# Windowed attention over half-blocks of 64 keys in eight array tiles, with the value products in two turns around a score batch

## Chip, cores and metric

The kernel runs on one core of one Trainium2 chip. The metric is the device time of one execution in microseconds (us), median over the runs. One run of the kernel before (388.53 us, the first of all) is left out. The profile of a run is one more execution, and its span (first to last instruction) is some 2 us shorter than the time.

## The reference

A layer norm of x (2048 rows of 512), then two branches whose results are added to x: attention with 32 heads of 16 dimensions, where a query sees itself and the 255 keys before it, and a gated product without a nonlinearity.

```python
xn = _layernorm(x)
qkv = (xn @ wqkv)                                  # 512 -> 3*512, 32 heads of 16
scores = einsum("bhqd,bhkd->bhqk", q, k) * 16**-0.5
mask = (i - j >= 0) & (i - j < 256)                # i: query, j: key
p = softmax(where(mask, scores, -1e9))
a = einsum("bhqk,bhkd->bhqd", p, v) ... @ wo
h = (xn @ w_gate) * (xn @ w_up)                    # 512 -> 1792
return x + a + h @ w_down
```

## The kernel before

The sequence is cut into four chunks of 512 rows (T), the heads into four quarters (c) of eight heads, and those into two parities (par) of four heads (e). TensorE is kept busy by interleaving attention with "fillers", the large products (projections, gate, up, down, output projection), all 128x128 by 512 columns. A schedule on cost estimates decides how many fillers stand between two score batches.

A score batch multiplies blocks of 128 keys with the queries that can see them, for four heads at once: each head has 16 or 32 rows of the array (a 32x128 tile) and writes its 512 columns to a PSUM bank of its own. Per chunk, quarter and parity there are six key blocks with 1, 2, 3, 3, 2 and 1 query blocks, packed into three batches. ScalarE takes the exp of a whole batch (128 x 2048), GpSimd zeroes what the mask hides, block by block. A value product then takes three batches: 128 keys deep, 17 columns per head (16 values and a column of ones for the softmax sum), four heads side by side (128x32 tiles).

```python
GROUPS = (            # (key block, first query block, last, column)
    ((-2, 0, 0, 0), (0, 0, 2, 128)),
    ((-1, 0, 1, 0), (2, 2, 3, 256)),
    ((1, 1, 3, 0), (3, 3, 3, 384)),
)

def scores(self, T, c, par, i):
    S = self.ps_s.tile([128, 4, 512], F32, tag="S", name="S")          # four banks
    for kb, q0, q1, col in parts:
        for e in range(4):
            nc.tensor.matmul(S[:, e, col:col + n], lhsT=K[rows of e, ..128 keys..],
                             rhs=Q[rows of e, .. n queries ..], tile_position=(32 * e, 0), ...)
    nc.scalar.activation(out=P[:, :, lo:hi], in_=S[:, :, lo:hi], func=ACT.Exp, scale=0.25)
    # ... one gpsimd.affine_select per block on the diagonal (q == kb) or the window's end (q == kb + 2)

def values(self, T, c, par):
    acc = self.accb                                                    # a bank of its own
    # ... for each of the three batches, key block and e:
    #     matmul(acc[32e:32e+17, queries], lhsT=V[128 keys, 17], rhs=P, tile_position=(0, 32e))
    nc.vector.transpose(out=at, in_=acc[:])
    nc.vector.reciprocal(out=rz[:], in_=at[:, :, 16])
    nc.vector.tensor_tensor(out=self.on[:, :, par, :], in0=at[:, :, 0:16], in1=rz..., op=ALU.mult)
    if par == 1:
        nc.vector.transpose(out=self.OT[T][:, c, :], in_=self.on...)

for g, s in enumerate(steps):            # 96 batches
    fill(-1, g)
    self.scores(*s)
    values(g - LAG)                      # LAG = 2: values of the batch two before, if it was the last of three
    fill(total * done_w / sum(weight), g)
```

The large products go through three more PSUM banks (`ps_m`), which VectorE or ScalarE must empty before they are used again.

The softmax here doesn't subtract the row's maximum and nothing guards it: scores larger than these inputs give would overflow.

## Time and profile before

| | before |
|---|---|
| time, median of the runs | 285.11 us |
| span of the profile | 282.7 us |
| TensorE busy | 96% |
| VectorE, ScalarE, GpSimd busy | 66%, 65%, 58% |
| first score batch starts | 13.64 us |
| last score batch starts | 265.43 us |

Part 1 of the page of the kernel before: busy us, share of the span and instruction count of each engine.

```profile
PE 270.2 (96%) x2380; PEld 113.9 (40%) x2396; DVE 186.5 (66%) x338; ACT 182.9 (65%) x121; POOL 162.6 (58%) x284
```

Busy time of TensorE (PE) is no proof of a full array, since matmuls are pipelined: the record of a full-array matmul lasts 0.38 us. The start times tell more: the next one starts 0.216 us after it. The stretch view of the kernel before, from the first scores to the first scores of chunk 1, and from there to the last score batch (columns: stretch, length, then busy us and count for each engine):

```profile
13.60:66.05 52.45, 48.67 (x400) 19.59 (x401) 42.67 (x77) 36.56 (x28) 31.61 (x56) 1.00 0.41 122
66.05:265.40 199.35, 197.03 (x1811) 80.93 (x1823) 133.48 (x237) 136.80 (x79) 124.00 (x208) 1.00 0.06 15
```

TensorE has hardly a gap after 66 us, and no other engine comes near. Before that, in the first chunk, it loses nearly 4 us (stretch minus busy time), and VectorE is 81% busy.

The timeline of TensorE in the kernel before, one score batch and one value product (columns: start, us, engine, line, operation, tiles, shapes, count):

```profile
127.72 0.40 PE L222 MATMUL S<-Q,Ko 32*128 32x256 bf16 x8
128.04 0.83 PE L255 MATMUL accb<-P,V 128*17 128x128 bf16 x24
128.81 1.47 PE L164 MATMUL vp<-Wqkv,xnT 128*128 128x512 bf16 x6
```

From start to start the batch takes 0.33 us and the value product 0.77. Another 0.09 us passes between the last full-array matmul's 0.216 us and the first score matmul (read from single starts). The second column is not the cost: it includes the tail of the pipeline. Streaming itself takes 0.417 ns per column, an estimate; so 512 columns take 0.213 us, 128 take 53 ns and 64 take 27 ns.

The first chunk, where a batch follows a value product without fillers between, in the timeline of the kernel before:

```profile
35.27 0.29 PE L222 MATMUL S<-Q,Ko 32*128 32x256 bf16 x4
35.49 0.67 PE L255 MATMUL accb<-P,V 128*17 128x384 bf16 x16
36.74 0.40 PE L222 MATMUL S<-Q,Ko 32*128 32x384 bf16 x8 [0.59 <-ACT P L230]
```

The product of 35.49 should end the step at 36.09. The next batch waits until 36.74 because the exp of the batch before still reads the score banks.

### The profile page before, as it was taken

What the parts mean: (1) busy time and instruction counts of PE and PEld (TensorE: products, weight loads), DVE (VectorE), ACT (ScalarE), POOL (GpSimd) and SP (SyncE); (2) the same over time, 40 slices, a digit from 0 to 9 for tenths busy, and PEclk for the clock granted to TensorE, in tenths of its full rate; (3) what the DMA queues carried; (4) which work ended last, traced back from release to release, by engine and by line L of the source; (5) the groups of instructions that cost most, each with busy time, mean ns of one, the idle gap of its engine ahead of it and who ended that gap; (6) DMA issues with size and microseconds to landing.
All of it is one profiled execution on the core that took longest, in us unless ns stands there. A gap on an engine that the chain in (4) does not pass through costs nothing.

```text
span 282.7 us, 5799 instructions
## 1 busy us (share of the span) xinstructions
PE 270.2 (96%) x2380; PEld 113.9 (40%) x2396; DVE 186.5 (66%) x338; ACT 182.9 (65%) x121; POOL 162.6 (58%) x284
## 2 busy tenths in 40 slices
PE   7999898989999999999999999999999999999994
PEld 6433333334344434443444344434434444433441
DVE  6377989958675777775853688875753367877122
ACT  3667666687576666668757676767776666756601
POOL 5146666765676665556586756465656566655510
PEclk9999999999999999999999999999999999999999
DMA  6999510100022100000011110000001000000002
GB/s 199 379 371 349 98 21 19 21 0 3 0 58 56 40 0 2 1 2 0 2 39 38 56 21 0 2 2 1 2 0 37 21 21 1 2 0 2 0 0 74
DMA packets 17161, 13.73 MB, mean 49 GB/s; under 512 B 7024, under 2 KB 17136, under 8 KB 17136
## 3 DMA queue, kind: packets, MB, share of 16 engines
q1 hardware_dynamic: 16848, 13.18, 15.5%
q8 instruction: 18, 0.29, 0.4%
q10 hardware_dynamic: 288, 0.20, 0.2%
q14 instruction: 7, 0.06, 0.1%
HBM read 9.70 MB, written 2.10 MB: 42 GB/s over the span
## 4 chain that ended last, share of the span: by engine, by line
PE 79%; DVE 10%; ACT 5%; issue 2%; DMA 1%; POOL 1%; ACTq 0%; DVEq 0%
PE psd L308 17%; PE gp L282 15%; PE up L293 14%; PE S L222 10%; PE accb L255 7%; PE qkp L176 6%; ACT P L230 5%; PE psd L313 4%; PE vp L164 4%; DVE at L266 2%; DVE OT L272 2%; DVE on L269 1%; DVE Q L187 1%; DVE hT L297 1%; DVE K L181 1%
## 5 line engine op out<-in xcount | busy, mean ns | idle before, releaser
L230 ACT ACTIVATE P<-S 128x2048 bf16<-128x2048 f32 (+2 forms) x96 | 170.1, 1772 | 79.1 <-PE S L222 68.5
L235 POOL TENSOR_SCALAR_AFFINE_SELECT P<-P 128x512 bf16<-128x512 bf16 x128 | 82.4, 644 | 57.5 <-ACT P L230 57.5
L239 POOL TENSOR_SCALAR_AFFINE_SELECT P<-P 128x512 bf16<-128x512 bf16 x112 | 72.9, 651 | 39.8 <-ACT P L230 39.5
L282 PE MATMUL gp<-xnT,Wg 128*128 128x512 bf16 x224 | 59.7, 380 | 1.2 <-DVE hT L297 1.1
L293 PE MATMUL up<-xnT,Wu 128*128 128x512 bf16 x224 | 60.4, 380 | 0.2 <-DVE gsb L287 0.2
L308 PE MATMUL psd<-Wd,hT 128*128 128x512 bf16 x215 | 53.1, 380 | 1.4 <-issue 0.8
L266 DVE STREAM_TRANSPOSE at<-accb 128x512 f32<-128x512 f32 x32 | 22.8, 713 | 38.9 <-PE accb L255 38.8
L297 DVE TENSOR_TENSOR hT<-up,gsb 128x512 bf16<-128x512 f32 x56 | 38.4, 686 | 7.8 <-PE up L293 5.2
L287 DVE CAST gsb<-gp 128x512 bf16<-128x512 f32 x56 | 38.2, 683 | 6.4 <-PE gp L282 6.1
L282 PEld LDWEIGHTS <-Wg 128*128 128x128 bf16 x224 | 20.0, 98 | 27.7 <-issue 7.1
L308 PEld LDWEIGHTS <-hT 128*128 128x128 bf16 x224 | 20.3, 98 | 26.7 <-issue 5.2
L176 PE MATMUL qkp<-xnT,Wqkv 128*128 128x512 bf16 x128 | 30.7, 380 | 0.0
L293 PEld LDWEIGHTS <-Wu 128*128 128x128 bf16 x224 | 19.8, 98 | 26.0 <-issue 5.9
L255 PE MATMUL accb<-P,V 128*17 128x384 bf16 (+2 forms) x704 | 25.4, 276 | 0.0
L329 DVE TENSOR_TENSOR y<-psd,x 128x512 bf16<-128x512 f32 (+1 forms) x15 | 9.9, 665 | 22.8 <-PE psd L313 21.5
L222 PE MATMUL S<-Q,Ko 32*128 32x256 bf16 (+2 forms) x352 | 18.4, 275 | 2.0 <-ACT P L230 2.0
L222 PE MATMUL S<-Q,K 16*128 16x256 bf16 (+2 forms) x352 | 18.4, 275 | 1.0 <-ACT P L230 0.7
L255 PEld LDWEIGHTS <-V 128*17 128x17 bf16 x704 | 13.8, 90 | 8.7 <-issue 5.5
L176 PEld LDWEIGHTS <-Wqkv 128*128 128x128 bf16 x128 | 11.3, 98 | 14.6 <-issue 2.9
L181 DVE CAST K<-qkp 128x512 bf16<-128x512 f32 x16 | 11.0, 687 | 8.5 <-PE qkp L176 8.4
L313 PE MATMUL psd<-Wo,OT 128*128 128x512 bf16 x61 | 16.0, 379 | 0.5 <-issue 0.5
L269 DVE TENSOR_TENSOR on<-at,rz 128x256 bf16<-128x256 f32 x32 | 15.4, 482 | 1.1
(39 smaller groups left out, 138.9 us busy)
## 6 DMA issues: line engine op xcount, KB each, us to landing
Wg<-in_B_w_gate_dram SPq DMA_DIRECT2D x2, 896.0 KB, 10.8
Wu<-in_B_w_up_dram SPq DMA_DIRECT2D x2, 896.0 KB, 11.9
Wd<-in_B_w_down_dram SPq DMA_DIRECT2D x1, 1792.0 KB, 16.4
out_dram<-y SPq DMA_DIRECT2D x14, 128.0 KB, 1.7
Wqkv<-in_A_wqkv_dram SPq DMA_DIRECT2D x3, 512.0 KB, 5.7
x<-in_A_x_dram SPq DMA_DIRECT2D x1, 1024.0 KB, 11.1
x<-in_A_x_dram SPq DMA_DIRECT2D x1, 512.0 KB, 11.1
Wo<-in_A_wo_dram SPq DMA_DIRECT2D x1, 512.0 KB, 16.3
```

The lines of the kernel that those rows point to most:

```text
L176: nc.tensor.matmul(ps[:], lhsT=self.Wqkv[:, k, lo:lo + 128], rhs=self.xnT[T][:, :, k, :], start=(k == 0), stop=(k == 3))
L222: nc.tensor.matmul(S[:, e, col:col + n], lhsT=(self.Ko if par else self.K)[U][rows, c, 128 * j:128 * j + 128], rhs=self.Q[T][rows, c, 128 ...
L230: nc.scalar.activation(out=P[:, :, lo:hi], in_=S[:, :, lo:hi], func=ACT.Exp, scale=0.25)
L235: nc.gpsimd.affine_select(out=P[:, :, j:j + 128], in_=P[:, :, j:j + 128], pattern=[[0, 4], [1, 128]], compare_op=ALU.is_ge, fill=0.0, base ...
L239: nc.gpsimd.affine_select(out=P[:, :, j:j + 128], in_=P[:, :, j:j + 128], pattern=[[0, 4], [-1, 128]], compare_op=ALU.is_gt, fill=0.0, bas ...
L255: nc.tensor.matmul(acc[32 * e:32 * e + 17, 128 * q0:128 * q0 + n], lhsT=self.V[U][:, v, 8 * c + 2 * e + par, 0:17], rhs=P[:, e, col:col + ...
L266: nc.vector.transpose(out=at.rearrange("p b r -> p (b r)"), in_=acc[:])
L282: nc.tensor.matmul(ps[:], lhsT=self.Wg[:, k, 128 * f:128 * f + 128], rhs=self.xnT[T][:, :, k, :], start=(k == 0), stop=(k == 3))
L287: nc.vector.tensor_copy(out=self.gsb[:], in_=ps[:])
L293: nc.tensor.matmul(ps[:], lhsT=self.Wu[:, k, 128 * f:128 * f + 128], rhs=self.xnT[T][:, :, k, :], start=(k == 0), stop=(k == 3))
L297: nc.vector.tensor_tensor(out=self.hT[T][:, f, :], in0=ps[:], in1=self.gsb[:], op=ALU.mult)
L308: nc.tensor.matmul(self.psd, lhsT=self.hT[T][:, f, 128 * b:128 * b + 128], rhs=self.Wd[:, f, :], start=(f == 0), stop=False)
```

## The change

The aim is to spend fewer columns on keys outside the window, and to use the array in eight tiles at a time.

- Keys go in half-blocks of 64. One needs 320 query columns, where a block of 128 needs 384. Per chunk, quarter and parity that is 2560 columns of 64 keys, 2.5 full batches, where there were 3: 76 batches in all for 96 (batch Z serves both parities).
- Scores use 32x64 tiles: four heads times two half-blocks at once. Values use 64x32 tiles: four heads times two halves of 64 rows.
- The two row halves must not write to one PSUM bank at once. The Trainium skill, "TensorEngine Tiling (Array Packing)", Gotcha 1, says that different row tiles cannot access the same bank simultaneously. So both parities are computed together, in two turns: in turn 0 the even half-blocks write to the accumulator of parity 0 and the odd ones to that of parity 1, in turn 1 the other way round. A tiny ScalarE read of each accumulator (a "mark") makes turn 1 wait for the end of turn 0, and a score batch stands between to hide the wait.
- The accumulators are two of the (now four) rotating banks; the score banks are one lasting tile, cleared at the start and used for the last down sums.
- The masks are 64-row cuts on GpSimd; those of batch Y, parity 1, become multiplications on VectorE in chunks 1 to 3.

```diff
+STEPS = {            # (half-block, column, first query, queries); two in a step run side by side
+    "X": (((0, 0, 0, 320), (1, 0, 64, 320)), ((-2, 320, 0, 192), (5, 320, 320, 192))),
+    "Y": (((2, 0, 128, 320), (3, 0, 192, 320)), ((6, 320, 384, 128), (-3, 384, 0, 128)),
+          ((-4, 448, 0, 64), (7, 320, 448, 64))),
+    "Z": (((4, 0, 256, 256), (-1, 0, 0, 256)),),
+}
 ...
-        self.ps_a = pool("ps_a", 1, space=bass.MemoryType.PSUM)
-        self.ps_m = pool("ps_m", 3, space=bass.MemoryType.PSUM)
+        self.ps_m = pool("ps_m", 4, space=bass.MemoryType.PSUM)
 ... scores
+                        nc.tensor.matmul(S[64 * r:64 * r + 64, e, base + col:base + col + n],
+                                         lhsT=(self.Ko if pr else self.K)[U][rows, c, 64 * k:64 * k + 64],
+                                         rhs=self.Q[T][rows, c, q0:q0 + n], start=True, stop=True,
+                                         tile_position=(32 * e, 64 * r), skip_group_check=True)
 ...
+        if T and (kind, par) == ("Y", 1):
+            for late, blk in enumerate((P4[:, :, 0:6:5, :], P4[:, :, 4:8:3, :])):
+                nc.vector.tensor_tensor(out=blk, in0=blk, in1=m, op=ALU.mult)
+        else:
+            for r, late, b in edges:
+                self.cut(P4[64 * r:64 * r + 64, :, b, :], late)
 ... values(T, c, turn)
+                        r = h % 2
+                        par = r ^ turn
+                        nc.tensor.matmul(self.acc[par][32 * e:32 * e + 32, q0:q0 + n],
+                            lhsT=self.V[U][64 * r:64 * r + 64, v:v + 32], rhs=P[64 * r:64 * r + 64, ...],
+                            tile_position=(64 * r, 32 * e), skip_group_check=True)
+        if turn == 0:
+            for p in (0, 1):
+                nc.scalar.activation(out=mark[:], in_=self.acc[p][:, 256 - p:257 - p], func=ACT.Copy)
 ... run
-            self.scores(*s)
-            values(g - LAG)
+            if pair:
+                self.values(*steps[d][:2], 0)
+            self.scores(*s)
+            if pair:
+                self.values(*steps[d][:2], 1)
 ...
+            if pair:
+                divide(d, upto)      # two transposes with reciprocals, then two divisions, fillers between
```

## The prediction

> **What bounds the kernel now.** TensorE, nearly everywhere. By the stretch table it is busy 197.0 of the 199.4 us from 66 to 265; VectorE has 133.5 there, ScalarE 136.8, GpSimd 124.1. The granted clock is 0.998. In the timeline full-array 512-column matmuls start every 0.216 us, so the 928 of them take 200 us. The rest is attention. In a steady stretch (121 to 129 us) a score batch costs 0.09 us to enter from full-array matmuls, then 0.33 until the next form starts, though its 512 columns stream in 0.213. A value product takes 0.77 us, 0.64 of it 1536 columns. 96 batches and 32 products come to about 64 us. The first chunk (14 to 66 us) loses some 4 us more, 1.7 of it scores waiting for the exp (waits view).
>
> **What the change does to TensorE.** Half-blocks of 64 keys need 320 query columns instead of 384: per chunk and quarter 5 batches for 6, and 1280 columns per value turn for 1536. Eight tiles work at once instead of four, so the columns per batch stay 512. The Trainium skill, "TensorEngine Tiling (Array Packing)", Key Properties, says that different tiles run in parallel and that changing the tiling mode drains the array. The trace agrees for four tiles (starts 3 ns apart, 0.1 us per change); for eight nothing here shows it. Tile matmuls double (704 to 1440 for scores, 704 to 1408 for values); at 3 ns per start that adds 0.02 us per batch, but pieces of 64 columns (27 ns) will wait for their weights (a 128-column piece took 61 ns, not 53).
> Estimates from these: batch 0.35, value turn 0.71 (0.57 in the first chunk), entry 0.09: 76 x 0.44 + 24 x 0.71 + 8 x 0.57 = 55 us. Saved: 9 us. Even batches should remove most of the first chunk's exp waits: 2 us.
>
> **Given back.**
> - Marks: the second value turn waits for two tiny ScalarE copies. 0.17 (matmul tail) + 0.12 + 2 x 0.17 + 0.05 = 0.68 us after the first turn, of which the score batch hides 0.47: 0.2 us, about 12 times, 2.5 us.
> - VectorE burst: two transposes with reciprocals together (1.9 us), two divisions, mask multiplies moved to it (about 14 us, an estimate), and accumulators take two of the four rotating PSUM banks. In gate/up stretches stalls: 2 us.
> - Start: clearing four banks, not one (0.48 us): VectorE +1.4 us, of which 0.45 lies before the first norm.
> - End: block 2's down sums wait for the last exp (0.7), the last two divisions outlast the filler matmuls (1.2), the split store saves 0.4: +1.5.
>
> **Off the path.** Exp falls from 170 to about 143 us. GpSimd stays equal: 384 cuts at 0.41 us (line through 0.29 at 128 and 0.64 at 512 elements) for 240 at 0.65.
>
> **Prediction.** 285.1 - 9.3 - 2 + 2.6 + 2 + 0.5 + 1.5 = about 280; I say 279.5 us, 8 in 10 within 274.5 to 284.5. Faster by over 2% 0.47, within 2% 0.48, slower 0.05.
>
> **What would show each step.** Matmul starts 3 ns apart, score batch near 0.35 us; value turn near 0.71; a wait of the second turn for the mark near 0.2; exp count 76; waits of gate/up for VectorE around the transposes; TensorE gaps before the last exp's end and the last output projections.
>
> **What would make it wrong.** Eight tiles not overlapping or a dearer change of form (a batch at 0.45 costs 8 us: no gain); marks queued behind other ScalarE work; dearer GpSimd cuts; or, to the good, marks and VectorE bursts fully hidden: 275.

## The result

| | before | after |
|---|---|---|
| time, median of the runs | 285.11 us | 280.78 us |
| span of the profile | 282.7 | 279.2 |
| TensorE busy | 270.2 | 264.3 |
| VectorE, ScalarE, GpSimd busy | 186.5, 182.9, 162.6 | 193.1, 159.6, 175.2 |
| last score batch starts | 265.43 | 259.06 |

The ratio is 0.9846 (95% interval 0.9827 to 0.9866). A ratio here is the mean time of one kernel's runs over that of the other's of the same rounds, so not quite the ratio of the medians. Executions over 1.5% slower than the fastest of the same kernel are left out of the means. (With the 388.53 us run the median of the kernel before is 285.22.) By the means the kernel is 4.4 us faster: inside the predicted range, "within 2%". Its own repetition on another chip gave 0.9861 (below, e0_after).

Part 1 of the page and the two stretches of the kernel after (first scores to the first scores of chunk 1, and on to the last score batch):

```profile
PE 264.3 (95%) x3866; PEld 126.5 (45%) x3886; DVE 193.1 (69%) x362; ACT 159.6 (57%) x133; POOL 175.2 (63%) x437
```

```profile
14.10:64.80 50.70, 46.81 (x665) 21.56 (x665) 39.55 (x74) 32.59 (x26) 39.80 (x100) 1.00 0.40 124
64.80:259.10 194.30, 191.03 (x2942) 88.58 (x2960) 140.84 (x261) 117.25 (x91) 128.08 (x311) 1.00 0.06 16
```

The later chunks are 5.1 us shorter, the first chunk only 1.8, and it still has some 4 us of gaps. Some matmul records are missing from this profile (of the full-array ones, by the gaps of whole 0.216 us steps); the repetition e0_after has all of them, and the sums below use it for chunks 1 to 3.

The timeline of the kernel after: a value pair around a score batch, and a plain batch of 24 matmuls.

```profile
116.95 0.75 PE L296 MATMUL acc<-P,V 64*32 64x320 bf16 x48
117.64 0.43 PE L246 MATMUL S<-Q,K 16*64 16x320 bf16 x24
118.05 0.74 PE L296 MATMUL acc<-P,V 64*32 64x320 bf16 x48
...
123.61 0.43 PE L246 MATMUL S<-Q,Ko 32*64 32x320 bf16 x24
123.97 2.76 PE L187 MATMUL vp<-Wqkv,xnT 128*128 128x512 bf16 x12
```

A plain batch takes 0.36 us to the next form, a turn 0.68. The batch inside a pair takes 0.41: the second turn waits only 0.06 us for its marks. The eight starts of a step are 3.3 ns apart (read from single starts).

Where TensorE waited, in the waits view (columns: us in total, times, longest). First the one line of the kernel before that the prediction named (1.7 us of it lie before 60 us), then the kernel after.

```profile
PE S L222 <- ACT P L230: 2.7, 6, 1.0
```

```profile
PE acc L296 <- DVE gsb L347: 2.1, 2, 1.2
PE wps L102 <- POOL ident L95: 1.4, 1, 1.4
PE up L353 <- DVE y L395: 1.0, 3, 0.6
PE S L371 <- DVE y L395: 0.9, 1, 0.9
PE psd L377 <- DVE OT L332: 0.9, 1, 0.9
PE S L246 <- ACT P L256: 0.9, 2, 0.5
```

The exp waits of the scores fell from 2.7 to 0.9 us, as predicted. But a new wait took their place: value products that wait for VectorE's copy of a gate product (gsb). The first one, in the timeline of the kernel after, all engines (the bracket at the end is the engine's idle time before the line and what ended it):

```profile
25.33 2.54 POOL L274 TENSOR_SCALAR_AFFINE_SELECT P<-P 64x256 bf16<-64x256 bf16 x6 [0.52 <-ACT P L256]
...
27.96 0.22 POOL L147 TENSOR_SCALAR ve<-mv 128x1 f32<-128x1 f32 x1
28.26 0.57 POOL L149 TENSOR_TENSOR rs<-ve,mhalf 128x1 f32<-128x1 f32 x1
...
28.54 0.31 PE L296 MATMUL acc<-P,V 64*32 64x320 bf16 x1
...
28.87 0.49 DVE L157 TENSOR_SCALAR xn<-x,mv,rs 128x512 bf16<-128x512 bf16 x1 [2.12 <-POOL rs L149]
29.28 0.67 DVE L347 CAST gsb<-gp 128x512 bf16<-128x512 f32 x1
...
30.00 0.63 PE L296 MATMUL acc<-P,V 64*32 64x320 bf16 x35 [1.16 <-DVE gsb L347]
```

Read it from below. The other 35 value matmuls start at 30.00, 1.47 us after the first, because the second accumulator takes the bank of a gate product, which VectorE copies out at 29.28. VectorE is late because the norm of the next chunk (xn) stands before the copy, and waited 2.12 us for GpSimd's rs. GpSimd was late because six cuts (2.54 us) stood before the norm's two small steps. Two more stalls of a value turn follow at 41.7 (1.3 us) and 55.2 (0.65 us).

The two stretch views say why GpSimd is late in this chunk: its busy time there rose from 31.61 us of 52.45 to 39.80 us of 50.70. There are 96 cuts of 0.43 us where there were 48 of 0.65, and none of this chunk's masks went to VectorE.

The end, in TensorE's timeline of the kernel after:

```profile
270.75 0.60 PE L371 MATMUL S<-Wd,hT 128*128 128x256 bf16 x4
272.26 0.38 PE L377 MATMUL psd<-Wo,OT 128*128 128x512 bf16 x1 [0.91 <-DVE OT L332]
272.47 0.38 PE L377 MATMUL S<-Wo,OT 128*128 128x512 bf16 x1
273.80 0.60 PE L371 MATMUL S<-Wd,hT 128*128 128x256 bf16 x4 [0.95 <-DVE y L395]
```

Two gaps, 1.9 us, that the kernel before does not have: after the last score batch it has none over 0.2 us. The first waits for the last transpose of the divisions. The second waits until VectorE has read block 2's sum, though the waiting matmuls write to other banks of the same tile. The skill, "PSUM — Partial Sum Buffer", section "PSUM bank collisions raise a hardware error", asks only for different banks or quadrants; so by the page this wait comes from the program's tracking of dependences by tile. No run here gives these sums separate tiles.

### The profile page after: what moved, and what is told of

The parts are those of the page before. It is cut to its first block, busy times and chain, and to the rows that moved or that the text cites. A ratio compares the mean times of both kernels' runs of the same rounds, so it can differ in the third digit from the quotient of the medians.

```text
span 279.2 us, 8943 instructions
## 1 busy us (share of the span) xinstructions
PE 264.3 (95%) x3866; PEld 126.5 (45%) x3886; DVE 193.1 (69%) x362; ACT 159.6 (57%) x133; POOL 175.2 (63%) x437
## 2 busy tenths in 40 slices
DMA packets 17175, 13.94 MB, mean 50 GB/s; under 512 B 7024, under 2 KB 17136, under 8 KB 17136
## 3 DMA queue, kind: packets, MB, share of 16 engines
q1 hardware_dynamic: 16848, 13.18, 15.5%
## 4 chain that ended last, share of the span: by engine, by line
PE 74%; DVE 10%; ACT 6%; POOL 5%; issue 3%; another core or an unknown queue 0%; DVEq 0%; ACTq 0%
PE psd L371 15%; PE up L353 13%; PE gp L342 12%; PE S L246 9%; PE qkp L199 8%; PE acc L296 7%; ACT P L256 5%; PE vp L187 5%; POOL P L274 4%; PE psd L377 4%; PE S L371 1%; DVE gsb L347 1%; DVE y L395 1%; DVE P L262 1%; DVE hT L357 1%
## 5 line engine op out<-in xcount | busy, mean ns | idle before, releaser
L274 POOL TENSOR_SCALAR_AFFINE_SELECT P<-P 64x256 bf16<-64x256 bf16 x384 | 159.1, 426 | 77.8 <-ACT P L256 65.6
L256 ACT ACTIVATE P<-S 128x2048 bf16<-128x2048 f32 x76 | 142.8, 1879 | 68.4 <-PE S L246 63.8
L371 PE MATMUL psd<-Wd,hT 128*128 128x512 bf16 x188 | 45.8, 380 | 0.8 <-issue 0.6
L316 DVE STREAM_TRANSPOSE at<-acc 128x512 f32<-128x512 f32 x32 | 21.9, 685 | 33.9 <-PE acc L296 33.9
L296 PE MATMUL acc<-P,V 64*32 64x320 bf16 (+4 forms) x1440 | 23.9, 253 | 2.5 <-DVE gsb L347 2.1
L296 PEld LDWEIGHTS <-V 64*32 64x32 bf16 x1440 | 18.0, 91 | 11.8 <-DVE gsb L347 3.8
L262 DVE TENSOR_TENSOR P<-P,edge 128x512 bf16<-128x512 bf16 x24 | 11.9, 535 | 15.4 <-ACT P L256 15.4
L246 PE MATMUL S<-Q,Ko 32*64 32x320 bf16 (+3 forms) x720 | 17.1, 258 | 1.3 <-ACT P L256 0.9
L246 PE MATMUL S<-Q,K 16*64 16x320 bf16 (+3 forms) x720 | 17.4, 262 | 0.2
L246 PEld LDWEIGHTS <-Ko 32*64 32x64 bf16 x720 | 9.3, 103 | 14.6 <-issue 14.4
```

The source lines that it names most:

```text
L246: nc.tensor.matmul(S[64 * r:64 * r + 64, e, base + col:base + col + n], lhsT=(self.Ko if pr else self.K)[U][rows, c, 64 * k:64 * k + 64], ...
L256: nc.scalar.activation(out=P[:], in_=S[:], func=ACT.Exp, scale=0.25)
L274: self.nc.gpsimd.affine_select(out=blk, in_=blk, pattern=[[0, blk.shape[1]], [sign, 64]], compare_op=ALU.is_gt if late else ALU.is_ge, fil ...
L296: nc.tensor.matmul(self.acc[par][32 * e:32 * e + 32, q0:q0 + n], lhsT=self.V[U][64 * r:64 * r + 64, v:v + 32], rhs=P[64 * r:64 * r + 64, e ...
L316: nc.vector.transpose(out=at.rearrange("p b r -> p (b r)"), in_=self.acc[par][:])
L371: nc.tensor.matmul(ps, lhsT=self.hT[T][:, f, 128 * b:128 * b + 128], rhs=self.Wd[:, f, c0:c1], start=(f == 0), stop=False)
```

## The experiments

Theory after the traces: the tile shapes give 7 us on TensorE; the first chunk gives back its share through queues (GpSimd's cuts before a norm, VectorE's order before a bank); the end gives back 1.6 us; the marks cost little. Rivals: eight tiles do not really stream together; two banks lent to the accumulators are too many whatever VectorE does; VectorE's masks or bursts are the loss.

The runs came in three groups, each on a chip of its own. The kernel before took 284.82, 284.81 and 284.85 us there, so times of different groups may be compared too; ratios are to the kernel before of the same group. Each was timed in three rounds.

| run | time us | ratio | 95% interval |
|---|---|---|---|
| e0_after (the changed kernel) | 280.77 | 0.9861 | 0.9847 to 0.9876 |
| e1_norm_late | 278.35 | 0.9773 | 0.9759 to 0.9788 |
| e2_no_cuts_chunk0 (wrong result) | 277.90 | 0.9758 | 0.9743 to 0.9772 |
| e3_tail | 279.83 | 0.9831 | 0.9815 to 0.9848 |
| e4_head | 280.46 | 0.9847 | 0.9833 to 0.9862 |
| e6_turns_together | 300.22 | 1.0545 | 1.0500 to 1.0589 |
| e7_masks_pool | 279.47 | 0.9816 | 0.9802 to 0.9831 |
| e8_before_norm_late | 284.07 | 0.9978 | 0.9961 to 0.9995 |
| e9_divide_now | 285.55 | 1.0032 | 1.0017 to 1.0047 |
| e10_gate_on_act | 277.61 | 0.9750 | 0.9733 to 0.9766 |
| e11_best | 274.98 | 0.9659 | 0.9644 to 0.9673 |
| e12_even_scores (wrong result) | 279.72 | 0.9826 | 0.9812 to 0.9841 |

### e0_after: the changed kernel as an anchor

> The changed kernel itself again, as the anchor for runs on the same chip: 280.4 to 280.8 us, ratio to the kernel before 0.983 to 0.986.

280.77 us, ratio 0.9861: as expected in time, just above the expected ratio. It is the reference for all that follows.

### e12_even_scores: half of the score matmuls

```diff
                     for h, col, q0, n in step:
+                        if h % 2:
+                            continue
```

> Wrong result on purpose: the score matmuls of odd half-blocks are left out, so 720 of 1440 score matmuls go, and four tiles stream what eight did, each its own stream unchanged. Theory (eight tiles really stream at the same time, and a matmul costs only its start, about 3 ns): a batch falls from 0.357 to 0.33 to 0.345 us, the kernel by 0.5 to 2 us. Rival (tiles in one row group share a stream, or starts are dear): a batch falls by 0.1 us or more, the kernel by 7 us or more.

736 of 1440 score matmuls are left (the expectation said 720; chunk 0 has more even half-blocks than odd). A batch fell from 0.357 to 0.344 us (medians of single starts, batches between fillers) and the kernel by 1.05 us, 76 x 0.013 = 1.0. So the odd tiles stream beside the even ones, and 704 matmuls with their weight loads cost 1 us in all. This is the central step of the change, and it holds. It was shown for the scores alone; for the values the trace says the same (48 matmuls in 0.68 us).

### e1_norm_late and e2_no_cuts_chunk0: the first chunk

```diff
# e1: the norm of chunk 1 is applied one gate/up pair later, for chunk 1 alone
-                    out.setdefault(at + step * b + (0, 0, 1, 1)[k], []).append((0, f))
+                    out.setdefault(at + step * b + (0, 0, lag, lag)[k], []).append((0, f))
-            gu(T, norms(1, 1, 3) if T == 0 else {})
+            gu(T, norms(1, 1, 3, 2) if T == 0 else {})
# e2 alone: no cuts in chunk 0
-            for r, late, b in edges:
+            for r, late, b in edges if T else []:
```

> The norm apply and transpose of chunk 1 are issued one gate/up pair later. In the trace of the changed kernel the first value pair (28.5 us) stalls 1.5 us inside its first turn: GpSimd does six cuts before the norm's scale, VectorE waits 2.1 us for the scale, the gate evacuation behind it comes late, and the accumulator's PSUM bank is free late. Theory A (that chain is the cause of the first stall, the other two at 41.7 and 55.2 us come from a VectorE that is two groups behind): the first stall goes, the other two stay; 280.8 becomes 279.3 to 279.8. Rival B (two banks of four lent at once are the cause whatever VectorE waits for): all three stalls stay, 280.8. Rival C (all three are the GpSimd chain): 3.4 us come back, 277.4.

> Wrong result on purpose: chunk 0 gets no mask cuts, so GpSimd is nearly free until 60 us. Theory A: only the first of the three stalls of value turns in chunk 0 goes (1.3 to 1.5 us), the other two (1.3 and 0.65 us) stay, because there VectorE is two groups behind on its own work; about 279.4. Rival C (GpSimd delays all three): about 277.4. Rival B (bank loan alone): 280.8.

e1 took 278.35 us, 2.4 us below e0_after: more than theory A expected, less than rival C. In its timeline the first pair no longer stalls:

```profile
28.33 0.63 PE L296 MATMUL acc<-P,V 64*32 64x320 bf16 x36
28.89 0.42 PE L246 MATMUL S<-Q,K 16*64 16x320 bf16 x20
```

The turn takes 0.56 us where it took 2.03. The second pair stalls 0.89 us instead of 1.25, the third 0.46 instead of 0.65. In e2, with no cuts at all, the first and third stalls are gone and the second is still 0.98 us; at 277.90 us it came near the number of rival C and not that of theory A. The stalls make up 2.4 of its 2.9 us. So the first stall is the chain over GpSimd, as theory A says; the third depends on GpSimd too, which theory A had wrong; the second does not. Rival B falls: the two banks were lent in all these runs, and stalls went.

### e10_gate_on_act: the second stall

```diff
+        if T == 0 and f % 3 == 2:
+            nc.scalar.activation(out=self.gsb[:], in_=ps[:], func=ACT.Copy)
+        else:
             nc.vector.tensor_copy(out=self.gsb[:], in_=ps[:])
```

> The late norms of e1_norm_late, and in chunk 0 every third gate evacuation (the one right after a norm's statistics) moves from VectorE to ScalarE. In e1_norm_late the second value pair still stalls 0.9 us inside its first turn, because the gate evacuation that frees its bank stands behind an up product (0.69) and the statistics (0.69 and 0.18) on VectorE, though that gate was done 1.4 us before. Theory A (order on VectorE): stalls of value turns in chunk 0 fall from 1.3 us in e1_norm_late to under 0.4; the kernel about 1.0 us below e1_norm_late. Rival B (ScalarE is no better, its exp of 1.88 us blocks the copy): within 0.3 us of e1_norm_late, or above it.

With the edit of e1 in it: 277.61 us, 0.74 below e1. The second stall is gone (the turn takes 0.56 us at 40.17 us in its trace), so what held it was the order on VectorE. The third became 0.70 us instead of 0.46, so the stalls left were 0.70 and not under 0.4. The trace of e10 shows what the third now waits for:

```profile
50.41 3.92 POOL L274 TENSOR_SCALAR_AFFINE_SELECT P<-P 64x256 bf16<-64x256 bf16 x9
...
53.06 0.22 PE L296 MATMUL acc<-P,V 64*32 64x64 bf16 x7 [0.50 <-POOL P L274]
```

It is no longer a bank but a cut: the last matmuls of the turn wait for GpSimd. In e1 they did so too (0.18 us by the same view). The turn starts 0.80 us earlier in e10 than in e1 (51.95 against 52.75), the cut releases it only 0.56 us earlier (53.06 against 53.62), and 0.24 us is what the stall grew.

### e8_before_norm_late: the same edit in the kernel before

> The late norm apply of e1_norm_late, put into the kernel before the change. There a batch brings GpSimd one or two cuts of 0.65 us, not six of 0.43, and VectorE waited for the norm's scale only 1.5 us in all (4.7 after the change). Theory (the loss is the change's own: its bursts of cuts): at most 0.7 us faster than the kernel before. Rival (any kernel with this order loses it): 2 us faster, as e1_norm_late against the changed kernel.

284.07 us, 0.8 us less than the kernel before, just over the 0.7 us that the theory allowed. The same edit gave 2.4 us in the changed kernel. So about two thirds of that loss is the change's own; by the interval of e8 alone (0.1 to 1.1 us), from a half to nearly all.

### e6_turns_together: no score batch between the turns

```diff
-            if pair:
-                self.values(*steps[d][:2], 0)
             self.scores(*s)
             if pair:
+                self.values(*steps[d][:2], 0)
                 self.values(*steps[d][:2], 1)
```

> Both value turns come after the score batch, so nothing hides the two marks between them. From the trace of the changed kernel: matmul tail 0.17, ScalarE start 0.12, two marks 0.23 together, return 0.05 make 0.57 us after the last stream of the first turn; with the score batch between, the wait seen is only 0.06. But the marks may also wait for the exp of that score batch, which now stands before them on ScalarE and lasts 1.88 us. Theory: if the marks wait for the exp, about 1.6 us more in each of 15 pairs, 20 to 27 us slower; if only the bare round trip is exposed, 15 x 0.35 to 0.45 = 5 to 7 us slower. Rival (the order is unimportant because TensorE has slack): within 1 us of the changed kernel.

300.22 us, 19.5 us slower, just under the 20 to 27 expected. Its four runs scatter from 298.59 us (granted clock 0.998) to 301.87 (0.987), so up to 1.6 us of this may be clock. The timeline of e6_turns_together shows why:

```profile
87.54 0.75 PE L296 MATMUL acc<-P,V 64*32 64x320 bf16 x48
87.73 1.88 ACT L256 ACTIVATE P<-S 128x2048 bf16<-128x2048 f32 x1 [1.14 <-PE S L246]
89.51 0.23 ACT L306 ACTIVATE mark<-acc 128x1 f32<-128x1 f32 x2
...
89.79 0.75 PE L296 MATMUL acc<-P,V 64*32 64x320 bf16 x48 [1.49 <-ACT mark L306]
```

The marks stand behind the exp on ScalarE, which runs its instructions in order (the skill, "TensorE: Matmul & The Clock Gate", section "Architectural detail: the array is 16× 32×32, not 1× 128×128", calls ScalarE and VectorE strict FIFO; this trace agrees). The waits view counts 21.4 us of value matmuls waiting for marks, in 15 waits. The place of the score batch between the turns therefore does two things: it hides the mark, and it puts the mark before the exp in ScalarE's queue. The bare round trip cannot be read from this run.

### e7_masks_pool: the masks of batch Y back on GpSimd

```diff
-        if T and (kind, par) == ("Y", 1):
+        if False:
```

> The 24 mask multiplies of VectorE go back to GpSimd as 96 cuts more (0.43 us each, 41 us, to 216 us busy in all), VectorE loses 12 us. Theory A (both engines have slack in chunks 1 to 3, the cuts of the four first batches are done before the values): within 0.7 us of the changed kernel. Rival B (GpSimd becomes late, values wait for the last cuts): 3 us or more slower, with waits of value matmuls for GpSimd in the trace. Rival C (VectorE was the limit in gate and up stretches): 1 us or more faster.

279.47 us, 1.3 us faster: rival C, against theory A. The timeline of e0_after suggests that more than the 12 us of VectorE work counts:

```profile
224.44 0.93 DVE L262 TENSOR_TENSOR P<-P,edge 128x512 bf16<-128x512 bf16 x2 [3.19 <-ACT P L256]
...
225.29 0.68 DVE L395 TENSOR_TENSOR y<-psd,x 128x512 bf16<-128x512 f32 x1
...
226.02 1.02 PE L353 MATMUL up<-xnT,Wu 128*128 128x512 bf16 x4 [0.63 <-DVE y L395]
```

VectorE sits idle for 3.19 us, because the mask multiply at the head of its queue waits for the exp. The copy of a finished down sum (y) stands behind it, and the up product waits for that bank. Over the kernel VectorE idles 15.5 us at these masks, in 12 waits, and TensorE pays for some of it. In e7 VectorE has no such waits, TensorE's waits for y in the chunks are gone, and GpSimd took 480 cuts of 0.42 us and made four value turns late, by 0.03 to 0.09 us each. The edit takes away the idling and the work at once, so no run separates the two: an edit that issues the same multiplies later could.

### e9_divide_now: the divisions without fillers between

```diff
             for par in (0, 1):
-                if upto is not None:
-                    fill(min(spent + 4, upto), g)
                 self.divide(T, c, par)
```

> The divisions follow the two transposes at once, no filler matmuls' evacuations between. Theory A (a VectorE burst of 3.6 us in a row with two of four banks lent stalls the gate and up groups): 12 to 15 pairs lose 0.2 to 0.6 us each, 3 to 8 us slower than the changed kernel. Rival B (the burst is hidden by the ring of banks): within 0.7 us.

285.55 us, 4.8 us slower: theory A. The VectorE burst that the prediction feared is real, and the change already contains the remedy. The longest of the new waits is a gate product that waits 1.40 us for VectorE.

### e3_tail and e4_head

```diff
# e3: all matmuls before the stores
-        fill(spent + 12, -1)
+        fill(10 ** 9, -1)
+        assert n == len(work)
         for b in range(3):
             self.wo(T, b, (3,))
-            self.store(T, b, on_act=(b == 1))
-        fill(10 ** 9, -1)
-        assert n == len(work)
         self.wo(T, 3, (0, 1, 2, 3))
+        for b in range(3):
+            self.store(T, b, on_act=(b == 1))
# e4: the clearing of the score banks moves behind the norms of chunk 0
-        nc.vector.memset(self.S[:], 0.0)
+        self.nc.vector.memset(self.S[:], 0.0)          # in first_chunk(), after the last norm_apply
```

> At the end all remaining matmuls go before the stores, the leftovers of block 3 before the last output projections. Theory: the two TensorE gaps after 272 us (0.91 us for the last division's transpose, filled by the leftovers of some 0.6 us, and 0.95 us for the store's read of block 2, a wait within the one tile of the score banks) go: TensorE ends about 1.4 us earlier, the kernel 1.0 to 1.4 us earlier, 279.4 to 279.8. Rival: the end is bound by the stores (evacuations and the last landing), and the kernel stays within 0.3 us of 280.8.

> The clearing of the four score banks moves behind the norms of chunk 0. Theory: the first norm starts 0.4 us earlier (2.88 as before the change, against 3.28) and the first scores at 13.65 against 14.15 us; 280.3. Rival: the head is bound by the weights' landing, no change, 280.8.

e3 took 279.83 us, 0.9 less than e0_after (0.8 in the spans of the profiles), a little under the range expected. TensorE ended 1.55 us earlier (273.50 against 275.05), but the stores gave part back: block 2's sum and the two halves of block 3 lie in one tile, and their three readers were now put one after the other.

e4 took 280.46 us. In its profile the first scores start at 13.79 us, in e0_after, e1 and e3 at 13.94, so the clearing costs 0.15 us, not 0.45. As times, 0.9847 and 0.9861 have overlapping intervals: not resolved. The 0.5 us between the two profiles of before and after (13.64 and 14.15) is mostly variation from run to run: the same start gave 14.15 and 13.94 in two profiles of the changed kernel, and e8, which has the start of the kernel before, gave 14.05.

### e11_best: all mends together

> All mends together: late norms and the third gate on ScalarE in chunk 0, mask multiplies back on GpSimd, matmuls ahead of the stores at the end, the clearing behind the first norms. If their gains add up (3.2 for the first two against the changed kernel, 1.3 masks, 0.9 end, 0.15 head): 275.2, ratio to the kernel before 0.966. If they overlap: 276 to 277.

e1, e10, e7, e3 and e4 in one kernel: 274.98 us, correct, ratio 0.9659. The gains add up (280.77 - 3.2 - 1.3 - 0.9 - 0.15 = 275.2). It beats both kernels: 3.4% below the one before. Part 1 of its page and TensorE's waits, all of them:

```profile
PE 265.0 (97%) x3886; PEld 125.9 (46%) x3886; DVE 182.3 (67%) x334; ACT 161.5 (59%) x137; POOL 212.1 (78%) x533
```

```profile
PE wps L101 <- POOL ident L95: 1.4, 1, 1.4
PE S L246 <- ACT P L256: 0.9, 2, 0.5
PE acc L296 <- POOL P L274: 0.5, 1, 0.5
PE xTp L172 <- DVE xn L156: 0.3, 1, 0.3
```

What is left on TensorE is work, but for these 3.1 us and gaps too small for the view. The 0.5 us on GpSimd is the third stall of e10. Of the waits of the changed kernel for VectorE only the norm at the start remains.

## Why the prediction was right or wrong

The total came out within 1.3 us (279.5 against 280.78; the sum of the prediction's terms, "about 280", is even nearer). But four of its six terms were wrong by more than 1.5 us, two in each direction, and they cancelled: the hit is in part luck. Sizes are read from single start times; "us saved" counts negative.

| term | predicted | shown |
|---|---|---|
| attention on TensorE | -9.3 (64 to 55) | -7.0 (62.1 to 55.1) |
| first chunk's waits | -2 | about +0.2 |
| marks | +2.6 | +0.9 |
| VectorE burst, chunks 1 to 3 | +2 | about +0.3 |
| start | +0.5 | +0.15 shown by e4; +0.5 between the two profiles |
| end | +1.5 | +1.6 |

With +0.5 for the start the shown terms sum to -3.5, and the spans of the profiles differ by 3.5. Single terms are good to some 0.2 us.

1. **Attention.** What it costs after the change was right. Batch 0.35 predicted, 0.357 seen; turn 0.71 and 0.57 predicted, 0.68 and 0.56 seen; entry 0.09 as before. 76 x 0.357 + 24 x 0.68 + 8 x 0.56 + 78 x 0.092 = 55.1. The skill's two claims under Key Properties of "TensorEngine Tiling (Array Packing)", tiles in parallel and a drain at each change, hold for eight tiles by the trace and by e12. What failed is the size of the cost before: "about 64" took all 96 batches and 32 products at full length. In chunk 0, 16 of 24 batches have only 384 or 256 columns (0.27 and 0.22 us, not 0.33), and its eight products 0.60 us, not 0.77: 72 x 0.329 + 6.6 + 24 x 0.766 + 8 x 0.60 + 94 x 0.092 = 62.1 (6.6 is the sum of chunk 0's batches). The remark that small pieces would wait for their weights was wrong in size: steps of 128 and 64 columns took 56 and 28 ns, where streaming is 53 and 27 by the estimate above. (The profile has 1440 value matmuls; the prediction counted 1408.)
2. **First chunk.** "Even batches should remove most of the first chunk's exp waits: 2 us" failed as a gain. The exp waits did fall, but TensorE's gaps in that chunk are 5.2 us after (e0_after, marks left out) and were 5.1 before, counted from single starts between the first scores of this chunk and of the next. The step that was missed: in this chunk GpSimd's work per batch went from one to three cuts of 0.65 us (two on average) to six of 0.43, and the norm of the next chunk shares its queue. e1 and e2 show that chain for the first stall, e10 shows VectorE's order for the second. "GpSimd stays equal" was right in the sum over the kernel (155.3 us of cuts before, 159.1 after). It failed in the first chunk, where the batches fell from 24 to 16 but the cuts rose from 48 to 96, and GpSimd's busy time from 31.6 to 39.8 us; and it was blind to the burst.
3. **Marks.** 0.06 us per pair in chunks 1 to 3 and 0.075 in chunk 0, not 0.2. The two marks were costed one after the other (2 x 0.17). They overlap: together 0.23 us. The skill has this ("ScalarE: Activation LUTs", section "What ACT_TABLE_LOAD costs", last paragraph: back-to-back ACTIVATEs overlap by about 93 ns); here the second started 67 ns after the first, which took 172, an overlap of 105 ns. "Marks queued behind other ScalarE work", named as a danger, is what e6 makes happen, at 1.3 us per pair.
4. **VectorE.** TensorE's gaps in chunks 1 to 3 are about 2.7 us before and 3.0 after, marks left out. The burst is real (e9: 4.8 us) but is hidden by the fillers between the divisions, which the prediction did not credit. The masks do cost 1.3 us (e7), by the timeline mostly through idling at the head of the queue, which no run separates from their 12 us of work. Other waits went in return: from 67 to 258 us the waits view of the kernel before has TensorE waiting 1.0 us for VectorE in five waits (for hT, Q and gsb), that of e0_after 1.0 us in three, all for y. Why the five went was not tested.
5. **End.** Right in the sum but not in its parts: the wait of block 2 for the last exp (0.7) did not occur, the gap before the last output projections was 0.9 (1.2 predicted), and a gap of 0.95 us that was not foreseen came with one tile holding four banks. The end after TensorE's last matmul is 0.3 us shorter.
6. **GpSimd and ScalarE.** Cuts 0.426 us (0.41 predicted), exp 142.8 us (143 predicted): right.

Still open: why the five waits for VectorE in chunks 1 to 3 of the kernel before are gone, and how much of the 1.3 us of the masks is idling and how much work.

## What to carry to other kernels

Cost a schedule batch by batch where the first or last stage has other sizes than the steady one; a mean over all was off by 2 us here, more than the 1.3 us by which the whole prediction missed. Equal busy time on a helper engine does not mean equal effect: look at it stage by stage (here it rose by a quarter in the first chunk), at the largest burst that can stand before something urgent in the same queue, and at an instruction that waits at its head, since everything behind it waits too. When a change lends out buffers, list who must release each one, and in which order that engine will get to it; here five small moves, of order or from one engine to another, were worth 5.8 us (280.77 to 274.98), more than the 4.0 us of the change itself on the same chips (284.8 to 280.77).

## What the Trainium skill lacked or had wrong

- "TensorEngine Tiling (Array Packing)", Key Properties, tells of the drain at a change of tiling mode, without a figure. Here: 0.09 to 0.10 us beyond the last stream, in both directions and for four and eight tiles alike. Into the tile form the first tile matmul starts 0.309 us after the last full-array one, which streams for 0.216; out of it the first full-array matmul starts 0.173 us after the last matmul of 192 columns (80 ns by the estimate above) and, in the kernel before, 0.147 us after one of 128 (53 ns).
- The same page, Instruction Overhead, gives each matmul some 60 cycles. Added up over the matmuls of different tiles, that does not hold: eight matmuls with their weight loads started 3.3 ns apart, and a step of eight with 64 columns each took 28 ns in all. "TensorE: Matmul & The Clock Gate", section "Measured speedup vs the span model", with about 4 ns per tile, fits.
- "ScalarE: Activation LUTs" is right on the overlap of two small ACTIVATEs (105 ns here, 93 stated); the figure stands under a heading on table loads, where it is easily missed.
- We found no page with a duration for GpSimd's affine select: 0.426 us for 64 x 256 bf16, 0.644 for 128 x 512.
